# A two-part transformer layer on one core: another order of the same tasks, with the last token blocks loaded by SyncE

## The chip, the cores and the metric

The kernel runs on one core of a Trainium2 chip. A core has a matrix engine (TensorE, PE in the profile; its weight loads are shown apart as PEld), VectorE (DVE), ScalarE (ACT), GpSimd (POOL) and SyncE (SP), which only issues DMAs here. ACT issues some DMAs too. Each engine runs its own instructions strictly in their order; semaphores hold an instruction back until what it needs is there, and everything behind it on that engine waits too. Matmuls write to PSUM, which this kernel uses as eight banks of 128 x 512 f32. The metric is the device time of one execution in microseconds (us), lower is better.

## The reference

One sequence of 2048 tokens, width 640, all bf16. Part A is attention with a memory: layer norm, then q, k, v for 32 heads of 20; the tokens are cut into four segments of 512, and within a segment attention is causal.

```python
for s in range(N):                       # N = 4 segments of L = 512
    logits = einsum('bhqd,bhkd->bhqk', qs, ks) * scale + mask
    a_dot = einsum('bhqk,bhkd->bhqd', softmax(logits), vs)
    a_mem = einsum('bhld,bhde->bhle', phi(qs), M) / (einsum('bhld,bhd->bhl', phi(qs), z) + 1e-6)
    outs.append(g * a_mem + (1 - g) * a_dot)
    M = M + einsum('bhld,bhle->bhde', phi(ks), vs)
    z = z + einsum('bhld->bhd', phi(ks))
h = x + concat(outs) @ wo
out = h + silu(layernorm(h) @ w1) @ w2   # part B, 640 -> 1728 -> 640
```

Here phi(t) is t + 1 for positive t and exp(t) otherwise, and g is the sigmoid of one number for each head.

## The kernel before

The kernel declares 1,455 tasks (a group of matmuls, one copy, one DMA), each with what it reads and writes. Nothing is scheduled at run time. A long string, `ORDER`, lists the names of all tasks; `schedule` takes them one by one, and each is added to the end of the program of its engine. So the order of the list is, engine by engine, the order of the instructions. What the tasks of different engines owe each other (data and reused buffers) is turned into semaphore waits afterwards. A row of the list reads `name/engine:slots`: the letter after the stroke chooses the engine where there is a choice (A ACT, D DVE, G POOL, S SP), and the numbers choose the buffer, such as the PSUM bank. Two rules of the code matter:

```python
if name.startswith("fill"):
    ...
    t.name, t.eng, t.emit = "fill", PE, self.filler(a, int(name[4:]))
    order.append(t)
    continue
```

`fill30` puts thirty matmuls of 256 columns of zeros (L619) into PE's queue at that place. They read the zeros that `zpad` (L596, DVE) has written, and so wait for it, and nothing reads what they compute. They are no part of the declared tasks.

The segments are worked one after the other with overlap: while the scores of one segment are computed, the projections of the next and the second part of the one before run in between. Names carry the segment and the group or the block of 128 tokens. The ones that matter here:

- `x0`, `x1`, `x2`, `x4`, `x8`, `x12` (L579): loads of token blocks; `x12` loads the last four, into the buffers of blocks 0 to 3, when their outputs `out0` to `out3` (L1260) have been read out of them. `w_...` (L582): loads of weights.
- `iota` (L631, POOL) and `sel` (L633, DVE): the identity matrix, which the transposes on PE use.
- `n1_st`, `n1_r`, `n1_ap` (L747 and L750, L762 to L768, L774): statistics, inverse deviation and application of the first layer norm for a block. `n1_tp` (L783, PE) and `n1_te` (L792) transpose the first four blocks through PSUM; later blocks are transposed by DMA (`n1_tr`, L798). `n2_...`: the same for the second layer norm.
- `re_wq`, `re_wk` (L697 on ACT, L699 on DVE): one of five pieces of the query and key weights is put in the order of the heads.
- `pr` (L861, PE), `qe` (L869 on ACT, L870 on DVE): projections of queries and keys and their copies out of PSUM. `pr041x` is segment 0, piece 4, keys (1), first half (x). `ex` (L876), `pha` (L883) and `phb` (L889) make phi of them.
- `vt` (L901): twelve SBUF-to-SBUF DMAs for each segment, which gather the heads of groups 5 to 7; the scores of these groups need all twelve.
- `v` (L826) and `ve` (L836 on ACT, L837 on DVE): values.
- `qk` (L938, PE): scores of a group of four heads, `e` (L950, ACT): their exponential (four heads in one instruction in segment 0, two elsewhere), `mk` (L961, POOL): the causal mask.
- `av` (L982, PE), `oe` (L995 on ACT, L997 on DVE), `tn` (L1011, L1015), `nm` (L1028 to L1030 in segment 0, L1042 to L1048 later), `ad` (L1056): values times weights, copy, transposition back with the part from memory, division, and sum.
- `kt` (L1096), `mz` (L1104), `ma` (L1129 to L1133), `mb` (L1140): the update of the memory; `kt` is a transposing DMA issued by SP, into one of two buffers.
- `ot` (L1157), `wo` (L1165), `rs` (L1173): output projection and residual. `h1` (L1200, tail L1194), `th` (L1209), `s` (L1215), `h2` (L1242), `o` (L1255), `out` (L1260): the second part and the store.

Of the kernel before, what the change touches and what calls it, by code (L numbers as in the profile page):

```python
# [371 lines left out]
n1_st7:4 n1_st8:6 n1_r8/G n1_r7/D lsc2 lsc3 pr000y:4 qe000y/A qk3x0:0 e3x0:3 mk3x_0 vt02/A mk2x_256 vt05/S vt07/A
pr021y:7 qe021y/D pha031:1 epsg1 vt010/S vt011/S mk3x_256 pr020y:5 pr011y:6 qe011y/A vt04/S pr010y:4 qe010y/D qe020y/A
qk4x0:0 e4x0:5 mk4x_0 mk4x_256 phb031 n1_st11:2 vt06/A vt08/S vt09/S v00:6 ve00/A:0 qk0yb0:2 e0yb0:4 n1_st9:1
n1_st10:0 vt00/A vt03/S mk0yb_0 n1_tr5:0 kt00:1 n1_r11/D ex021:0 mk0yb_256 ex011:2 v01:0 qk1yb0:2 e1yb0:6 mk1yb_0
n1_r10/G ve01/D pha021:0 phb021 kt02:0 mk1yb_256 v03:6 ve03/D n1_ap11:2 n1_ap7:3 n1_tr7 n1_ap6:0 av4x:0 av0x:1
# [15 lines left out]
e8a0:6 av6y:4 pha111:1 e8a2 mk8a_0 oe6y/D:0 ex140:0 phb140 th0_8_0:0 qk8e0:0 e8e2:1 av4y:6 oe4y/D:1 mz03:7 e8e0
ma03/D:4 mk8e_0 mb03:0 mk8e_256 tn4y:6 nm4y:3 kt12:0 ex141:1 av7y:4 oe7y/D:1 tn6y:7 nm6y:0 qk8b0:0 e8b2:4 tn7y:4
nm7y:3 ot3 ot2 s0_8_0 pr130:6 qe130/D:0 e8b0 mk8b_0 mk8b_384 vt19/S pha130:0 qk9a0:2 e9a2:5 pr131:7 qe131/D vt12/S
vt11/S mz04:0 vt18/S n1_tr10:0 kt10:1 ma04/D:1 e9a0 mb04:0 mk9a_0 n1_tr8 vt110/S n1_tr11 h1_0_2_0:1 th0_2_0:1 vt15/S
qk9b0:4 e9b0:0 s0_2_0 pha131:0 h1_0_11_0:2 th0_11_0:0 s0_11_0 h1_0_0_0:0 th0_0_0:1 s0_0_0 e9b2 mk9b_0 h1_0_9_0:3
# [5 lines left out]
n2_st2:7 n2_r2/G qk12b0:1 e12b2:2 pr220:0 e12b0 qk13a0:3 qe220/D:0 mz13:7 ma13 n2_ap2:2 n2_tr2 e13a2:3 e13a0 mk13a_0
mk12b_0 mk12b_384 kt11:0 av11:2 tn9:0 v20:6 oe11/A:0 qk12e0:2 nm9:1,0 ve20/A:0 e12e0:0 mz10:0 kt14:1 e12e2 ma10
mk12e_0 ad9 n2_ap3:0 n2_tr3 v21:6 ve21/D qk13b0:0 e13b0:1 pr211:4 e13b2 mk13b_0 mk13b_384 pr210:5 qe211/D:0 ex211:2
mk12e_256 tn11:6 nm11:3,1 ad11 qe210/A qk14a0:1 e14a2:4 e14a0 mk14a_0 pr231:0 pha211:2 qe231/D:0 ex210:0 pr200:5
ex231:1 qk14b0:0 e14b2:6 e14b0 mk14b_0 mk14b_384 qe200/D:0 phb211 av13:4 oe13/D:0 ex200:2 v23:6 ve23/D h1_0_8_1:5
th0_8_1:1 qk14e0:0 e14e2:1 s0_8_1 mz11:4 ma11 e14e0 mk14e_0 mk14e_256 tn13:6 pr201:5 qe201/A tn10:2 pha200:0
h1_0_7_1:1 th0_7_1:0 nm13:3,1 ad13 mb10:0 qk15a0:4 e15a2:3 e15a0 mk15a_0 phb200 s0_7_1 pr221:0 qe221/A av14:1 av12:6
nm10:0,0 ad10 qk15b0:2 e15b2:4 vt20/S:0 vt26/S e15b0 mk15b_0 mk15b_384 vt29/S oe14/D:0 vt23/S tn14:0 oe12/D:1 nm14:3,0
pr241:7 qe241/D:0 pha201:1 mb11:0 ad14 ex201:2 h1_0_12_1:6 th0_12_1:1 qk16b0:0 e16b0:2 s0_12_1 tn12:4 nm12:0,1  # L410
h1_0_4_1:7 th0_4_1:0 s0_4_1 phb201 e16b2 mk16b_0 mk16b_384 h1_0_10_1:6 h1_0_0_1:0 av15:1 th0_0_1:1 s0_0_1 pha221:0
th0_10_1:0 s0_10_1 pha210:0 qk16a0:2 h1_0_6_1:7 oe15/A:0 tn15:0 mb13:0 ex221:2 phb221 kt22:0 e16a2:6 e16a0 ad12
nm15:0,0 ad15 ot6:0 ot7 ot4 pr240:6 h1_0_5_1:4 th0_6_1:0 qk16e0:0 mb12:0 qe240/D th0_5_1:1 s0_6_1 e16e0:5 s0_5_1 e16e2
mk16e_0 phb210 ex240:2 pha220:0 pha231:0 phb231 pr230:5 qe230/D vt25/S vt28/S ot5 vt27/S vt22/S pha240:0 vt210/S
vt211/S mk16a_0 vt21/S vt24/S mk16e_256 ex220:0 v22:6 ve22/D qk17b0:0 e17b2:3 phb240 h1_0_13_1:4 th0_13_1:1
h1_0_11_1:5 s0_13_1 th0_11_1:0 s0_11_1 phb220 e17b0 mk17b_0 mk17b_384 pha230:0 wo6:6 rs6 qk18b0:2 av16:0 oe16/D:1
# [901 lines left out]
```

## Time and profile before

| | us |
|---|---|
| median of 3 runs (lowest to highest) | 302.56 (302.05 to 302.67) |
| the profiled execution, own time | 303.2 |
| its span | 301.4 |
| ACT busy | 222.4 |
| POOL busy | 141.8 |

The span runs from the first to the last instruction of the profiled execution; 1.8 us of its time lie around it. A row of the timeline reads: start, length, engine and line, operation, tile written and tile read, shape, count, and in brackets how long the engine had been idle and what ended that. A row of waits reads: engine, tile and line, what released it, us in total, times, longest. ACTq and SPq are the queues in which those engines issue DMAs. `PT` is the tile of the exponentials, `stt` that of the statistics, `sT` that of the second part's activations (and, at first, of the raw weights); `w_sb` stands for several tiles of one shape in memory, the queries and keys of segment 0 among them.

### The profile page before, as it was taken

The numbers are of one execution on the slowest core, as the hardware profiler recorded it, in microseconds if no ns is written. First come the engines' busy times: TensorE is split into PE (matmuls) and PEld (weight loads), VectorE is DVE, ScalarE is ACT, GpSimd is POOL, SyncE is SP. The second block draws the span as 40 slices with busy tenths as digits, with TensorE's granted clock in tenths as the row PEclk, the third lists the DMA queues.
The fourth block names the chain that finished last, engine by engine and source line by source line (L and its number), as shares of the span: only waits on it lengthen the run. The fifth ranks groups of instructions, "written<-read, shape, count | busy, mean of one in ns | idle before, by whom it ended". The sixth has DMA issues, their size and how long they took to land.

```text
span 301.4 us, 7468 instructions
## 1 busy us (share of the span) xinstructions
PE 289.2 (96%) x2991; PEld 172.0 (57%) x3014; DVE 217.9 (72%) x510; ACT 222.4 (74%) x298; POOL 141.8 (47%) x272
## 2 busy tenths in 40 slices
...
GB/s 258 362 361 121 106 63 127 107 8 171 97 84 69 73 10 18 43 93 61 74 125 36 79 29 2 39 79 62 65 67 25 0 44 45 105 50 24 0 28 61
DMA packets 49250, 24.66 MB, mean 82 GB/s; under 512 B 39168, under 2 KB 47616, under 8 KB 49216
## 3 DMA queue, kind: packets, MB, share of 16 engines
...
## 4 chain that ended last, share of the span: by engine, by line
PE 75%; ACT 11%; DVE 5%; DMA 4%; issue 2%; SPq 1%; POOL 1%; ACTq 0%
PE ps_all L1242 21%; PE ps_all L1200 14%; PE ps_all L861 9%; ACT PT L950 8%; PE ps_all L1165 7%; PE ps_all L938 7%; PE ps_all L982 6%; PE ps_all L826 6%; DMA x_tok<-in_A_x_dram 3%; DVE stt L747 2%; PE ps_all L1011 2%; PE ps_all L1015 2%; SPq L901 1%; PE ps_all L1104 1%; DMA w_sb<-w_sb 1%
## 5 line engine op out<-in xcount | busy, mean ns | idle before, releaser
L950 ACT ACTIVATE PT<-ps_all 128x1024 bf16<-128x1024 f32 (+2 forms) x144 | 155.3, 1124 | 16.8 <-PE ps_all L938 15.7
L961 POOL TENSOR_SCALAR_AFFINE_SELECT PT<-PT 128x512 bf16<-128x512 bf16 x128 | 81.9, 645 | 70.5 <-ACT PT L950 67.6
L1242 PE MATMUL ps_all<-w_sb,sT 128*128 128x320 bf16 (+2 forms) x462 | 64.6, 295 | 0.0
L1200 PE MATMUL ps_all<-hT,w_sb 128*128 128x512 bf16 (+1 forms) x315 | 60.2, 335 | 1.0 <-issue 0.7
L1209 ACT ACTIVATE th<-ps_all 128x512 f32<-128x512 f32 (+2 forms) x70 | 33.6, 508 | 35.6 <-PE ps_all L1194 16.8
L1242 PEld LDWEIGHTS ps_all<-w_sb,sT 128*128 128x128 bf16 x462 | 43.1, 98 | 19.1 <-issue 3.0
L1215 DVE SCALAR_TENSOR_TENSOR sT<-th,ps_all 128x512 bf16<-128x512 f32 (+2 forms) x70 | 37.9, 561 | 18.5 <-ACT th L1209 17.8
L1200 PEld LDWEIGHTS ps_all<-hT,w_sb 128*128 128x128 bf16 x325 | 30.2, 98 | 25.3 <-issue 1.7
L1255 DVE SCALAR_TENSOR_TENSOR x_tok<-ps_all,x_tok 128x640 bf16<-128x640 f32 (+3 forms) x18 | 13.4, 749 | 23.1 <-PE ps_all L1242 23.0
L747 DVE BATCH_NORM_STATS2 stt<-x_tok 128x6 f32<-128x320 bf16 x64 | 27.9, 477 | 2.7 <-DMA x_tok<-in_A_x_dram 2.4
L1165 PE MATMUL ps_all<-wo_sb,oT 128*128 128x320 bf16 x160 | 24.1, 299 | 0.1
L982 PE MATMUL ps_all<-PT,Vx 128*32 128x256 bf16 (+3 forms) x576 | 23.5, 287 | 0.6 <-POOL PT L961 0.5
L1056 POOL TENSOR_TENSOR otok<-on 128x320 bf16<-128x320 bf16 x24 | 19.0, 792 | 5.9 <-DVE on L1048 5.8
L768 POOL TENSOR_TENSOR rst<-rst,eps_c 128x1 f32<-128x1 f32 x32 | 18.6, 583 | 5.6 <-DVE rst L762 3.8
L870 DVE CAST QK<-ps_all 128x512 bf16<-128x512 f32 x23 | 15.8, 686 | 6.9 <-PE ps_all L861 6.7
L1048 DVE TENSOR_TENSOR on<-ps_all,rd 128x640 bf16<-128x640 f32 x24 | 19.8, 825 | 0.8
L765 POOL TENSOR_TENSOR rst<-mvt,eps_c 128x1 f32<-128x1 f32 x23 | 4.9, 212 | 30.5 <-DVE mvt L750 28.1
L1165 PEld LDWEIGHTS ps_all<-wo_sb,oT 128*128 128x128 bf16 x160 | 14.9, 98 | 7.2 <-issue 1.9
L982 PEld LDWEIGHTS ps_all<-PT,Vx 128*32 128x32 bf16 x576 | 12.3, 96 | 10.9 <-issue 5.0
L826 PE MATMUL ps_all<-wv_sb,xT 128*128 128x320 bf16 x120 | 18.3, 299 | 0.1
L861 PE MATMUL ps_all<-xT,wqr 128*128 128x512 bf16 x71 | 17.7, 380 | 0.3 <-issue 0.2
L997 DVE TENSOR_SCALAR oTs<-ps_all,lsc 128x512 bf16<-128x512 f32 (+1 forms) x25 | 15.8, 640 | 2.9 <-PE ps_all L982 2.7
...
## 6 DMA issues: line engine op xcount, KB each, us to landing
...
out_dram<-x_tok SPq DMA_DIRECT2D x9, 160.0 KB, 1.8
...
out_dram<-x_tok ACTq DMA_DIRECT2D x6, 160.0 KB, 2.0
...
```

The source lines that it names most:

```text
L747: T.add(DV, lambda e, hh=hh: e.bn_stats(out=stt[:, s, 6 * hh:6 * hh + 6], in_=xb[:, 320 * hh:320 * hh + 320]), reads=R((xa, xsub)), writes ...
L826: fns.append(lambda e, c=c, hh=hh: e.matmul(bank(ps, hh)[:, 0:320], lhsT=xT_[:, c, 128 * i:128 * i + 128], rhs=wv_sb[:, c, 320 * hh:320 * ...
L861: fns = [lambda e, kc=kc: e.matmul(bank(ps)[:, lo:hi], lhsT=wt[:, kc, c, :], rhs=xT_[:, kc, lo:hi], start=(kc == 0), stop=(kc == NC - 1)) ...
L938: fns.append(lambda e, j=j, o=o, r=r, q0=q0, q1=q1, qa=qa, ka=ka: e.matmul(ps_all[:, o:o + q1 - q0], lhsT=ka[32 * r:32 * r + DH, 128 * j:1 ...
L950: T.add(AC, lambda e: e.activation(out=pt[:, pta.slot, q0:q0 + nq, 0:width], in_=sc3[:, b0:b0 + nq, 0:width], func=ACT.Exp, scale=SCALE), ...
L961: T.add(PO, lambda e: e.affine_select(out=v, in_=v, pattern=[[0, 4], [1, 128]], compare_op=ALU.is_ge, fill=0.0, base=0, channel_multiplier ...
L982: fns.append(lambda e, j=j, r=r, h=h, pa=pa, pt=pt, co=co, q0=q0, ji=ji: e.matmul(bank(po)[32 * r:32 * r + 32, q0:hi], lhsT=Vx[:, vx.slot, ...
L1165: fns.append(lambda e, c=c, hh=hh: e.matmul(bank(ps, hh)[:, 0:320], lhsT=oT[:, c, 128 * i:128 * i + 128], rhs=wo_sb[:, c, 320 * hh:320 * h ...
L1200: fns = [lambda e, c=c: e.matmul(bank(ps)[:, lo:hi], lhsT=w1_sb[:, c, 128 * f:128 * f + 128], rhs=hT[:, c, lo:hi], start=(c == 0), stop=(c ...
L1209: T.add(AC, lambda e: e.activation(out=th[:, tha.slot, lo:hi], in_=bank(ps)[:, lo:hi], func=ACT.Tanh, scale=0.5), reads=R((ps, [0])), writ ...
L1215: T.add(DV, lambda e: e.scalar_tensor_tensor(out=sT[:, f, lo:hi], in0=th[:, tha.slot, lo:hi], scalar=1.0, in1=bank(ps)[:, lo:hi], op0=ALU. ...
L1242: fns.append(lambda e, f=f, t0=t0, fr=fr, hh=hh, n=n: e.matmul(bank(pa, hh)[:, 0:n], lhsT=sT[:, f, t0:t0 + 128], rhs=w2_sb[:, fr, c0 + 320 ...
```

## The change

Only `ORDER` is replaced. Both lists hold the same 1,455 declared tasks, and both compute the exponential of segment 0 four heads at a time. What differs:

- the order, mostly by exchanges of near neighbours; on PE the largest moves are among the last blocks of the second part (`h2_9` to `h2_14`, and the `h1_3` tasks);
- the zero matmuls: 32, 15 and 4 instead of 30, 7 and 4; the second group stands ahead of `pr020x` instead of behind it;
- on DVE `sel` stands ahead of `zpad`; on POOL `mt2 halfc mt0 mta2 mtb2 mm10` stand ahead of `iota`, where `mt2 vpad1 mt1 vpad0 mt0` stood;
- the engine of 46 tasks: 15 go from ACT to DVE (`re_wk1`, `qe031x`, `qe000y`, `oe4x`, `oe0x`, `oe2x`, `ma00`, `qe210`, `qe301`, `qe341`, `qe340`, `ve31`, `oe25`, `oe26`, `oe30`), 12 from DVE to ACT (`re_wq3`, `qe030x`, `qe040y`, `qe031y`, `qe021y`, `ma02`, `qe241`, `oe18`, `ve30`, `qe300`, `qe331`, `oe27`), 9 between DVE and POOL (all `n1_r` or `n2_r`), and ten DMAs change their queue: `w_w2_0`, `w_w2_2`, `vt111`, `out0`, `out1`, `out2`, `x12`, `out11` from ACT to SP, `out5`, `out13` from SP to ACT.

Of the two lists, the rows at the start, those that the text speaks of, and the last two:

```diff
-zpad:0 x0:7 mt2 vpad1 mt1 vpad0 mt0 iota epsg0 mt3 halfc sel x1:3 mta3 epsc w_q:0 x2:5,0 w_k1 mta0 mtb0 w_k0 mtb3 mm2
-w_wv0:0 x4:1,2,4,6 w_wv1 warm n1_st0/D:1,0 n1_r0/G n1_st1/D:6 n1_r1/D n1_ap0:0 mm9 n1_ap1:1 n1_st2/D:2 n1_r2/G mta1
-mm8 re_wq2/D:0 n1_st3/D:0 n1_r3/G w2z/G:0 w_wo:0 beta w_w2_4 mm11 x8/S:8,9,10,11 mta2 mtb1 mtb2 mm5 mm3 re_wq0/D mm4
-mm10 w_w1_2:0 n1_ap2:3 mm6 mm1 re_wk0/D:0 w_w1_1 n1_ap3:2 re_wq4/D mm7 re_wq3/D re_wk3/D re_wk2/D fill30:0 n1_st5:3
-n1_r5/G mm0 n1_tp0:6 re_wk4/D n1_st4:7 n1_r4/G w_w1_0 w_w2_5 w_w1_3 n1_te0/A:0 n1_ap5:0 n1_tp1:4 n1_te1/A pr020x:2
-re_wq1/A fill7:1 pr010x:0 qe020x/A:0 re_wk1/A qe010x/A:0 w_w1_4 pr000x:4 qe000x/A:0 n1_tp2:5 n1_te2/A pr001x:7
-qe001x/A n1_tp3:2 n1_te3/A pr011x:1 qe011x/A qk0x0:4 e0x0:0 mk0x_0 pr040x:0 pr001y:2 qe001y/A pr030x:3 qe040x/A:0
...
-phb001 n1_st6:5 pr031y:3 pr041y:2 qe041y/A pr030y:0 qe030y/A qe031y/D ex031:0 pr041x:6 qe041x/D vt01/S:0 n1_r6/D
...
-oe4x/A:1 qk7x0:2 av2x:6 n1_tr4 tn4x:7 n1_r9/D oe0x/A:0 e7x0:5 n1_tr6 oe2x/A:1 nm4x:0 pha011:2 mk7x_0 mk7x_256 v02:0
...
-av1x:0 fill4:6 tn0x:7 av7x:6 oe7x/A:0 oe1x/D:1 tn1x:0 nm2x:1 qk0ya0:2 av5x:1 nm0x:0 nm1x:3 oe5x/D:1 av3x:7 tn7x:6
-nm7x:2 oe3x/D:0 av6x:1 tn5x:6 nm5x:3 mz00:0 tn3x:7 e0ya0:5 oe6x/A:1 qk1ya0:2 nm3x:1 tn6x:6 nm6x:0 ma00/A:0 mb00:0
-phb041 n1_ap8:0 ot1:0 v10:0 mz02:7 ot0 kt01:1 e1ya0:0 qk2ya0:2 ve10/A av0y:6 oe0y/D:1 ma02/D:3 n1_ap9:3 mb02:0 kt03:0
-e2ya0:2 v12:0 ve12/D qk2yb0:2 wo1:6 e2yb0:1 mk2yb_0 qk3ya0:0 e3ya0:3 w_w2_0/A av1y:4 oe1y/A:0 rs1 mk2yb_256 n2_st1:5
...
-s0_3_0 th0_10_0:0 s0_10_0 h1_0_1_0:4 qk7yb0:0 mk6yb_256 pr140:5 qe140/D e7yb0:2 w_w2_2/A w_w2_3/S th0_1_0:1 s0_1_0
...
-mk9b_384 vt17/S mz12:1 ma12 vt111/A h1_0_13_0:2 th0_13_0:0 th0_9_0:1 s0_9_0 qk10a0:4 e10a0:3 s0_13_0 n1_tr9 e10a2
...
-mk11b_0 mk11b_384 phb111 h2_1_2 h2_1_3 o1 qk12a0:0 av10:4 wo2:5 out0/A e12a0:5 oe10/D:1 e12a2 ad8:0 mk12a_0 out1/A rs2
...
-mk19b_0 n2_tr4 mk19b_384 mk18a_0 h2_2_1 h2_2_2 h2_2_3 o2 h2_3_0:0 tn17:2 nm17:3,1 n2_tr5 ad17:0 qk19a0:4 out2/A
...
-tn18:0 nm18:2,0 ad18 mz14:7 ma14 mb14:0 kt23:1 h1_1_10_0:6 tn16:4 oe19/A:0 th1_10_0:0 x12/A s1_10_0:0 nm16:2,1
...
-out15_1/A h2_12_2 h2_12_3 o12 out12/S h2_14_3 o14 out14/S h2_15_0_0:2 h2_15_1_0 h2_13_0:0 h2_13_1 h2_13_2 h2_13_3 o13
-out13/S h2_15_2_0 h2_15_3_0 o15_0 out15_0/S h2_15_0_2:3 h2_15_1_2 h2_15_2_2 h2_15_3_2 o15_2 out15_2/S
+x1:3 x0:7 mt2:0 halfc mt0 mta2 mtb2 w_q:0 mm10 iota mt1 mta0 mtb0 mm2 mm4 x2:5,0 w_k1 w_k0 w_wv1:0 sel zpad warm vpad0
+epsc n1_st0/D:1,0 n1_r0/G n1_st1/D:6 n1_r1/D mm6 n1_ap0:0 n1_ap1:1 epsg0 n1_st2/D:2 n1_r2/G re_wq2/D:0 mt3 mta3
+n1_st3/D:0 n1_r3/G w2z/G:0 mtb3 mm8 mm11 w_wv0 x4:1,2,4,6 mta1 w_wo:0 beta w_w2_4 x8/S:8,9,10,11 w_w1_2:0 mm0 mtb1 mm5
+n1_ap2:3 re_wq0/D mm3 re_wk0/D:0 mm9 w_w1_1 mm1 vpad1 n1_ap3:2 w_w1_4 w_w2_5 re_wk1/D re_wq4/D re_wk2/D re_wk3/D
+re_wk4/D n1_st4:7 n1_r4/G n1_st7:4 n1_r7/G n1_st6:5 n1_r6/G mm7 n1_st5:3 n1_r5/G w_w1_0 fill32:0 n1_tp0:2 n1_te0/A:0
+n1_tp1:0 n1_te1/A fill15:4 re_wq1/A w_w1_3 pr020x:0 re_wq3/A pr010x:6 qe020x/A:0 n1_tp2:2 qe010x/A:0 n1_ap4:1 n1_te2/A
+pr000x:5 qe000x/A:0 pr001x:1 qe001x/A n1_tp3:6 pr011x:4 qk0x0:0 n1_ap7:3 n1_ap6:0 n1_te3/A qe011x/A pr040x:5 e0x0:0
+mk0x_0 mk0x_256 qe040x/A:0 pr001y:6 pr030x:7 qe001y/A qk1x0:0 e1x0:1 zf0 zf1 mzc9 mzc8 mzc0 mzc11 mzc1 mzc5 mzc3 mzc6
+mzc2 pr021x:4 qe021x/A pr031x:5 lsc0 mzc4 lsc1 pr040y:6 qe040y/A mk1x_0 qk2x0:0 qe030x/A:0 qe031x/D e2x0:2 mk2x_0
+mk1x_256 mk2x_256 pr030y:4 pr031y:6 qe031y/A pr041y:7 mzc7 pr041x:0 qe030y/A qe041y/A qe041x/D pha031:1 ex001:1
+pha001:2 vt011/S:0 ex031:0 n1_ap5:2 phb031 pr000y:1 qe000y/D qk3x0:2 e3x0:3 vt02/A mk3x_0 mzc10 epsg1 n1_st8:6 vt08/S
...
+n1_tr6 qk1yb0:2 e1yb0:6 ex021:0 kt00:1 ve03/D n1_r8/D mk1yb_0 mk1yb_256 n1_tr4 av0x:1 av4x:0 oe4x/D:1 tn4x:6 av2x:7
+oe0x/D:0 qk7x0:2 e7x0:5 mk7x_0 nm4x:0 phb021 kt02:0 mk7x_256 n1_ap9:2 oe2x/D:1 n1_tr7 v02:0 qk5x0:2 e5x0:0 mk5x_0
+mk5x_256 ve02/D v11:6 tn2x:0 qk6x0:1 e6x0:2 mk6x_0 pha011:2 mk6x_256 n1_ap11:0 phb011 ve11/D:1 av1x:5 oe1x/D:1 fill4:6
+nm2x:1 tn0x:6 av7x:7 tn1x:5 nm0x:0 qk0ya0:0 nm1x:3 mz00:4 oe7x/A:0 pha041:0 kt01:1 ma00/D:0 mb00:0 av5x:6 av3x:7
+tn7x:5 oe5x/D:1 tn5x:4 av6x:6 e0ya0:5 oe3x/D:0 tn3x:7 nm7x:2 oe6x/A:1 qk1ya0:0 nm5x:3 nm3x:1 tn6x:6 nm6x:0 ot1:0 v10:4
...
+e2yb0:1 wo1:6 w_w2_0/S mk2yb_0 mk2yb_256 qk3ya0:0 e3ya0:3 ve12/D av1y:4 oe1y/A:0 rs1 n2_st1:5 n2_r1/G tn0y:7 nm0y:1
...
+qk7yb0:0 w_w2_2/S w_w2_3/S pr140:6 s0_3_0 e7yb0:2 mk7yb_0 mk7yb_256 pha110:0 h1_0_6_0:4 th0_1_0:1 th0_6_0:0 qe140/D
...
+pha130:0 e8b0 mk8b_0 mk8b_384 qk9a0:2 e9a2:5 pr131:6 qe131/D vt14/S n1_tr10:0 vt18/S vt111/S vt11/S n1_tr11 n1_tr9
...
+h2_1_0:6 e10e0 ex110:0 kt13:0 o0 out0/S mk10e_0 phb110 qk11a0:0 e11a0:6 e11a2 mk11a_0 mk10e_256 wo3:4 ex111:2 rs3
...
+av10:4 oe10/D:1 pha111:2 n2_ap3:0 out1/S n2_tr3 wo2:6 e12a0 mk12a_0 rs2 phb111 qk12b0:2 e12b2:2 pr220:0 qe220/D:0
...
+e18a0:4 e18a2 mk18a_0 n2_ap5:3 n2_tr5 h2_2_1 h2_2_2 qk19b0:0 e19b2:3 e19b0 mk19b_0 h2_2_3 o2 out2/S h2_3_0:4 mk19b_384
+ad17:0 qk19a0:0 e19a2:2 e19a0 mk19a_0 h2_3_1 h2_3_2 h2_3_3 av18:7 oe18/A:0 qk20b0:0 o3 out3/S e20b0:5 e20b2 mz14:6
+ma14 mb14:0 mk20b_0 mk20b_384 kt23:1 tn18:4 av19:7 oe19/A:0 x12/S h1_1_10_0:6 th1_10_0:0 nm18:2,0 s1_10_0:0 pha241:0
...
+out13/A h2_14_0:6 h2_14_1 h2_14_2 h2_14_3 o14 out14/S h2_15_0_2:5 h2_15_1_2 h2_15_3_1 o15_1 out15_1/A h2_15_2_2
+h2_15_3_2 o15_2 out15_2/S
```

More of the change, by code (lines that the diff above doesn't have):

```diff
@@ L372 @@
[L372 to L376, printed above, removed]
@@ L392 @@
[L392 to L396, printed above, removed]
@@ L402 @@
[L402 to L416, printed above, removed]
@@ L422 @@
-e19a2:2 e19a0 mk19a_0 h2_3_1 h2_3_2 h2_3_3 o3 out3/S av18:7 qk20b0:3 e20b2:5 av19:2 e20b0 mk20b_0 mk20b_384 oe18/D:0
-tn18:0 nm18:2,0 ad18 mz14:7 ma14 mb14:0 kt23:1 h1_1_10_0:6 tn16:4 oe19/A:0 th1_10_0:0 x12/A s1_10_0:0 nm16:2,1
-qk21b0:0 e21b0:6 pha241:0 e21b2 ad16 mk21b_0 h1_1_4_0:7 h1_1_7_0:6 th1_4_0:0 s1_4_0 th1_7_0:1 s1_7_0 phb241 n1_st12:0
-n1_r12/G n1_st13:3 n1_r13/G qk20a0:2 e20a2:0 e20a0 mk20a_0 h1_1_12_0:1 th1_12_0:0 h1_1_1_0:0 th1_1_0:1 s1_1_0 qk20e0:4
-h1_1_5_0:3 e20e2:4 e20e0 mk20e_0 mk21b_384 mk20e_256 n1_ap12:1 n1_tr12:0 s1_12_0 th1_5_0:1 h1_1_11_0:2 th1_11_0:0
@@ new lines @@
+mk1x_256 mk2x_256 pr030y:4 pr031y:6 qe031y/A pr041y:7 mzc7 pr041x:0 qe030y/A qe041y/A qe041x/D pha031:1 ex001:1
+pha001:2 vt011/S:0 ex031:0 n1_ap5:2 phb031 pr000y:1 qe000y/D qk3x0:2 e3x0:3 vt02/A mk3x_0 mzc10 epsg1 n1_st8:6 vt08/S
+lsc2 vt04/S vt05/S phb001 lsc3 mk3x_256 pr020y:6 pr021y:7 qe021y/A qe020y/A pha021:0 pr011y:0 qe011y/A qk4x0:2 e4x0:5
+mk4x_0 pr010y:1 qe010y/D vt07/A mk4x_256 n1_st11:2 n1_st10:0 vt01/S vt00/A v00:6 n1_st9:1 ve00/A:0 qk0yb0:2 vt010/S
+e0yb0:4 vt09/S mk0yb_0 vt06/A n1_r11/G ex041:1 mk0yb_256 ex011:2 vt03/S v01:0 ve01/D n1_r9/D n1_tr5:0 n1_r10/D v03:6
```

124 lines of the change are left out of this document (72 added, 52 removed).

## The prediction

> **What bounds the kernel now.** I read the page's totals first, then the busy time by stretches, then who TensorE (PE) waited for in three stretches, and last the timeline of the first 20 us and of the places where PE waits.
>
> ```profile
> span 301.4 us, 7468 instructions
> PE 289.2 (96%) x2991; PEld 172.0 (57%) x3014; DVE 217.9 (72%) x510; ACT 222.4 (74%) x298; POOL 141.8 (47%) x272
> ...
> 13.00:42.00 29.00, 26.95 (x353) 17.41 (x351) 26.18 (x85) 27.69 (x40) 22.06 (x54) 1.00 0.70 184
> 42.00:82.00 40.00, 38.14 (x458) 21.94 (x460) 29.93 (x79) 38.30 (x46) 17.24 (x28) 1.00 0.45 102
> 82.00:150.00 68.00, 67.14 (x752) 39.77 (x759) 54.17 (x120) 61.23 (x84) 38.96 (x63) 1.00 0.36 59
> 150.00:170.00 20.00, 18.83 (x166) 8.80 (x170) 17.04 (x39) 17.34 (x24) 10.83 (x20) 1.00 0.30 71
> 170.00:302.00 132.00, 127.76 (x1204) 76.00 (x1206) 81.70 (x157) 71.40 (x95) 43.24 (x71) 1.00 0.21 44
> ```
>
> The rows by stretch give length, then busy time of PE, PEld, DVE, ACT, POOL. PE is the bound nearly everywhere: 96% of the span, and the same matmuls stand in both lists, the zero matmuls of the fills apart. So a new order can win only what PE now spends waiting, and can lose without limit. From 13 to 42 ACT (27.69 of 29.00) and DVE (26.18) run almost without a break beside PE; from 42 to 82 ACT does (38.30 of 40.00). The waits of PE, in the order 13 to 42 (two rows), 42 to 82 (one), 82 to the end (three):
>
> ```profile
> PE ps_all L938 <- DMA w_sb<-w_sb: 0.7, 1, 0.7
> PE ps_all L982 <- POOL PT L961: 0.5, 1, 0.5
> ...
> PE ps_all L938 <- ACT PT L950: 1.0, 4, 0.4
> ...
> PE ps_all L1104 <- DVE sT L1215: 0.9, 1, 0.9
> PE ps_all L1200 <- issue: 0.7, 4, 0.2
> PE ps_all L861 <- issue: 0.5, 3, 0.2
> ```
>
> What can be won after the head is thus about 0.7 + 0.5 + 1.0 + 0.9 = 3.1 us; the "issue" rows have no releaser and stay.
>
> **The head (0 to 20 us): a loss.** The new list puts `sel` (L633) ahead of `zpad` (L596) on DVE. `sel` waits for POOL's `iota`; the fills (L619) read `zpad`. Today's rows:
>
> ```profile
> 0.88 0.17 DVE L596 MEMSET zpad<- 128x128 uint32 x1 [0.88 <-PEq L1303]
> 1.11 5.66 PE L619 MATMUL ps_all<-zpad 128*128 128x256 bf16 x30 [1.11 <-DVE zpad L596]
> 2.44 0.23 POOL L631 IOTA iot<- 128x128 int32 x1
> 2.71 0.23 DVE L633 TENSOR_SCALAR ident<-iot 128x128 bf16<-128x128 int32 x1 [1.66 <-POOL iot L631]
> ...
> 1.10:5.34 4.24, 4.23 (x20) 3.00 (x21) 1.00 0.83 271
> ...
> 6.61 0.44 PE L783 MATMUL ps_all<-ident,xn_rot 128*128 128x128 bf16 x5
> 7.09 0.70 ACT L792 ACTIVATE hT<-ps_all 128x640 bf16<-128x640 f32 x1 [2.73 <-PE ps_all L783]
> 8.55 0.82 ACT L697 ACTIVATE wqr<-sT 128x400 bf16<-128x400 bf16 x2
> 8.87 0.71 PE L861 MATMUL ps_all<-hT,wqr 128*128 128x256 bf16 x5 [0.95 <-DVE wqr L699]
> 9.41 0.93 PE L619 MATMUL ps_all<-zpad 128*128 128x256 bf16 x7
> 10.18 1.25 PE L861 MATMUL ps_all<-hT,wqr 128*128 128x256 bf16 x10
> 11.12 0.73 ACT L869 ACTIVATE w_sb<-ps_all 128x256 bf16<-128x256 f32 x2
> 13.37 0.34 PE L938 MATMUL ps_all<-w_sb 20*128 20x256 bf16 x8
> 13.79 1.46 ACT L950 ACTIVATE PT<-ps_all 128x1536 bf16<-128x1536 f32 x1
> 18.08 1.45 ACT L950 ACTIVATE PT<-ps_all 128x1536 bf16<-128x1536 f32 x1
> 20.03 0.75 DVE L870 CAST w_sb<-ps_all 128x256 bf16<-128x256 f32 x2
> ```
>
> A fill costs 4.24 / 20 = 0.212 us until about 5.6 us, and later (9.41 to 10.18 for seven) 0.110 us: TensorE's clock is at half speed for its first 4.5 us of work, 1.11 to about 5.6. (The granted clock in that row, third from its end, reads 1.00 all the same; the spacing decides.) Ahead of `iota` POOL has seven operations today and six of like size in the new list, so `sel` stays near 2.5 to 2.7, `zpad` ends near 2.8, and the 32 fills start at 2.8 instead of 1.11. They stand ahead of the first transpose n1_tp0 (L783, now at 6.61) in PE's queue. Lower bound: the clock rises at the same instant as now, 5.6: 13 slow fills (2.8) and 19 fast (2.1) end at 7.7. Upper: all 32 are slow, 2.8 + 6.8 = 9.6. I take the middle by the nearest row, a slow stretch of the same 4.5 us: 21 slow (4.5), 11 fast (1.2), so n1_tp0 at 8.5, which is 1.9 us late.
>
> Behind it ACT copies both transposes (0.70 each), rearranges wqr (0.82, and re_wq3, of three pieces where today's has two, some 0.9 more), and copies four projections and a transpose (0.35 a projection from 0.73 for two): qk0x0, the first scores (L938), follows n1_tp0 by about 5.3 us, at 13.8 instead of 13.37. The second fill (15 instead of 7, 1.65 us) moves ahead of pr020x; it ends near 10.4, only 0.2 behind the second copy, and so costs next to nothing more. The third exponential, e2x0 (now 18.08 to 19.53), follows qk0x0 by three exponentials, a transpose copy, six projection copies and two small constants, some 7.0 us: it ends near 20.8, 1.3 us late. pr041x takes a bank from it, DVE's qe041x (the second cast of the 20.03 row, over at 20.78) ends near 22.0, and the SBUF copies `vt` (L901), which need it, start about 1 us late.
>
> From there to 42 us DVE is the tight engine. It was idle 29.00 - 26.18 = 2.8 us; the list gives it oe4x, oe0x, oe2x, ma00, re_wk1, qe031x and qe000y from ACT and takes re_wq3, qe030x, qe040y, qe031y and qe021y from it: net two more of about 0.4 to 0.5 us, 1 us, beside the 0.9 that it waits for qe041x. What is late next is v10, for whose PSUM banks PE needs DVE's nm5x:
>
> ```profile
> 39.39 1.52 PE L826 MATMUL ps_all<-wv_sb,xT 128*128 128x320 bf16 x10
> ```
>
> I put it at 40.4: **+1.0 us at 40 us**, bounds +0.2 (fills end at 7.7) and +2.1 (at 9.6). In this the repairs of this stretch are contained: av2x and tn4x go ahead of qk7x0 (which has the 0.7 of DMA wait), mz00 and tn5x ahead of av6x (the 0.5 for POOL); both only pass on a wait that grows. [...]
>
> **42 to 82 us: a gain.** ACT sets the pace here. The chain that ended last holds two pieces on it that are no arithmetic: the issue of w_w2_2 and that of vt111.
>
> ```profile
> 66.69 0.91 issue
> ...
> 79.15 0.40 ACTq L901
> ```
>
> Both go to SP (w_w2_0 and vt111 too; SP has room, its next work there is the `vt` copies of segment 1, some us later). That frees 0.91 + 0.40 = 1.3 us of ACT, but PE waits only 1.0 us for ACT's exponentials in the whole stretch, and two of the four waits lie ahead of 66 us. **-0.5 us**, bounds -1.0 and 0.
>
> **150 to 170 us, the last token blocks (x12): a gain.**
>
> ```profile
> 150.86 0.37 SPq L1260 DMA_DIRECT2D out_dram<-x_tok  x1
> 152.50 1.21 SPq L1096 DMA_TRANSPOSE phiKt<-phiK  x1
> ...
> 150.89 0.73 PE L982 MATMUL ps_all<-PT,Vx 128*32 128x512 bf16 x16
> 151.87 0.61 PE L1104 MATMUL ps_all<-Vx,phiKt 128*128 128x84 bf16 x8
> ...
> 153.60 0.40 ACTq L579 DMA_DIRECT2D x_tok<-in_A_x_dram  x1
> ...
> 159.79 0.89 DVE L747 BATCH_NORM_STATS2 stt<-x_tok 128x6 f32<-128x320 bf16 x2 [1.47 <-DMA x_tok<-in_A_x_dram]
> ...
> out_dram<-x_tok SPq DMA_DIRECT2D x9, 160.0 KB, 1.8
> ```
>
> On ACT x12 stands behind two exponentials and oe19 and is issued at 153.60. It may not go before out3, which reads the same buffers, has landed: 150.86 + 1.8 = 152.7. On SP it stands behind the transposing DMA kt23, which waits for mz14; mz14 (L1104) goes ahead of av19 (L982) and tn18 in PE's queue, by 151.87 - 150.89 = 1.0 us, so kt23 runs from about 151.5 to 152.7. Then x12 is issued at 152.8, 0.8 us earlier; DVE's wait of 1.47 shrinks to 0.7, and the 0.9 us that PE waits for DVE's sT behind it (mz23) nearly goes. **-0.8 us**, bounds -0.9 and 0 (kt23 not earlier: 152.50 + 1.21 = 153.71, as late as now). Behind x12 on SP stands n1_tr12, which needs x12 anyway.
>
> **The rest.** out0, out1 and out2 leave ACT, where PE hardly waits for it (82 to 150: PE 67.14 of 68.00 busy): nothing; without that cover 0.4 us each. The two lists end on the same last piece of block 15, its output on SP: nothing. In 82 to 302 a few hundred neighbours are exchanged; the waits they can open are not in the trace. From both sides: nothing, or as much as today's list shows between 13 and 42, 1.2 us and more; the row nearest is that this list, of the same kind, has 1.2 us of short gaps beside mz23 there. I take **+0.5**, with -0.3 to +1.3.
>
> Sum: +1.0 - 0.5 - 0.8 + 0.5 = +0.2 us. On the profiled execution, 303.2 us (span 301.4 and 1.8 around it), that is 303.4; it lies 0.6 above the median of the three runs shown, so against that median I forecast 302.56 + 0.2 = **302.8 us**: no change that can be told (0.2%, 0.6 us, is about what a measurement of this kernel can tell).
>
> **The rivals.** *The late clock loses more, and the list gives nothing back* (slower). Place: PE's queue at n1_tp0; the fills run slow to the end, +2.1 at 40 us; ACT's relief comes to nothing as DVE stays late (0), x12 gives -0.5: +1.6, and 304.2 us. It decides from a first transpose at about 9 us on. For it: nothing but `zpad` starts the fills, DVE has no room until 42 us. Against it: the slow stretch of 4.5 us. *The head costs almost nothing* (faster): clock up at 5.6, +0.2, ACT -1.0, x12 -0.9, the rest 0: -1.7, and 300.9 us. For it: PE waited 0.95 us for wqr at 8.87 and spent 0.77 on seven fills behind it, cover for a late start. Against it: PE would have to be left with almost no wait. *The x12 move does nothing*, since kt23 stays in front of it on SP: the forecast without -0.8, 303.6 us. For it the 1.21 us of kt23; against it mz14's earlier place.
>
> **Chances.** Forecast 0.42 (its own range 302.0 to 303.8: no change 0.24, slower 0.12, faster 0.06); first rival 0.25, all slower; second 0.23 (faster 0.22, no change 0.01); third 0.10 (slower 0.06, no change 0.04). Together faster 0.28, within 0.2% 0.29, slower 0.43. The range takes in both sides, 300.9 to 304.6.
>
> **What would show it.** The first fill at 2.8, n1_tp0 at 7.7 to 9.6 and the first scores at 13.4 to 15; v10 near 40.4. In 42 to 82 a smaller wait of PE for ACT's PT; x12 issued by SP at 152.8 plus the shift of that place, and the wait of L1104 for sT under 0.2. I am wrong if the fills start at 1.1, if PE's place at 40 us is unchanged though the fills are late, or if new waits of over 1.3 us stand after 82.

## The result, and the profile after

| | median, us (lowest to highest) | beside the kernel before, same chips | ratio, 95% |
|---|---|---|---|
| before | 302.23 (301.80 to 303.51), 7 runs | | |
| changed | 304.45 (303.52 to 305.21), 7 runs | +2.22 us | 1.0071 [1.0048, 1.0094] |

The changed kernel is slower, by 0.7%. 304.45 us lies in the predicted range, 300.9 to 304.6, which takes in the rivals too, but only 0.15 us from its end, and the prediction does not work that end out. It lies outside the 302.0 to 303.8 that the prediction gives its own forecast: 302.8 us and no change was wrong. The first rival's 304.2 us is nearer, partly by luck: of its reasons, fills that run slow to the end and 0.5 us won by x12 did not come.

The page's totals, then the busy time by stretches (length, then PE, PEld, DVE, ACT, POOL, granted clock, DMA share, GB/s) of the changed kernel:

```profile
span 302.7 us, 7496 instructions
PE 289.4 (96%) x3002; PEld 172.6 (57%) x3024; DVE 220.4 (73%) x509; ACT 220.9 (73%) x296; POOL 142.5 (47%) x275
```

```profile
42.00:82.00 40.00, 37.84 (x474) 21.78 (x477) 30.83 (x79) 38.41 (x47) 15.68 (x27) 1.00 0.49 94
82.00:150.00 68.00, 66.56 (x747) 39.19 (x749) 54.32 (x119) 62.03 (x85) 38.34 (x64) 1.00 0.31 59
```

PE is busy 37.84 of the 40 us and 66.56 of the 68, against 38.14 and 67.14 before: both stretches, the one where ACT was relieved too, have more gaps than they had.

The waits of PE, from 13.3 to 42 us (two rows), 42 to 82 (one) and 82 to the end (one):

```profile
PE ps_all L619 <- DVE Vx L837: 1.1, 1, 1.1
PE ps_all L1015 <- DVE oTs L997: 1.0, 2, 0.8
...
PE ps_all L938 <- ACT PT L950: 0.4, 1, 0.4
...
PE ps_all L1165 <- DVE Vx L837: 0.7, 1, 0.7
```

Before 42 us PE now waits for DVE, 1.1 us for a copy of values (L837) and 1.0 us for two copies of attention results (oTs, L997), where it waited for a DMA and for POOL before. The wait for ACT's exponentials from 42 to 82 is down from 1.0 to 0.4 us as foreseen, but that gained nothing there. Behind 82 us there is one new wait of over 0.3 us, for DVE's copy of values (L837), ahead of L1165. The wait of L1104 for sT is gone. The head, in the timeline:

```profile
2.06 0.23 POOL L631 IOTA iot<- 128x128 int32 x1
2.33 0.23 DVE L633 TENSOR_SCALAR ident<-iot 128x128 bf16<-128x128 int32 x1 [2.33 <-POOL iot L631]
2.53 0.17 DVE L596 MEMSET zpad<- 128x128 uint32 x1
2.75 5.83 PE L619 MATMUL ps_all<-zpad 128*128 128x256 bf16 x32 [2.75 <-DVE zpad L596]
8.42 0.72 PE L783 MATMUL ps_all<-ident,xn_rot 128*128 128x128 bf16 x10
14.00 0.34 PE L938 MATMUL ps_all<-w_sb 20*128 20x256 bf16 x8
...
21.07 0.42 DVE L870 CAST w_sb<-ps_all 128x256 bf16<-128x256 f32 x1 [0.92 <-PE ps_all L861]
...
41.00 1.52 PE L826 MATMUL ps_all<-wv_sb,xT 128*128 128x320 bf16 x10
```

The fills start at 2.75, the transposes at 8.4, the first scores at 14.0, qe041x ends at 21.5 and v10 (the last row) starts at 41.0. Two profiled executions cannot be set against each other as they are, though: that of before (303.2 us) lies 1 us above its kernel's median, and experiments 4 and 5 show what was in it.

### The profile page after: what moved, and what is told of

Same layout as the page of the kernel before. It is cut to its first block, busy times and chain, and to the rows that moved or that the text cites. A ratio compares the mean times of both kernels' runs of the same rounds, so it can differ in the third digit from the quotient of the medians.

```text
span 302.7 us, 7496 instructions
## 1 busy us (share of the span) xinstructions
PE 289.4 (96%) x3002; PEld 172.6 (57%) x3024; DVE 220.4 (73%) x509; ACT 220.9 (73%) x296; POOL 142.5 (47%) x275
## 4 chain that ended last, share of the span: by engine, by line
PE 80%; ACT 9%; DVE 7%; issue 2%; POOL 1%; POOLq 0%; ACTq 0%
PE ps_all L1242 20%; PE ps_all L1200 15%; PE ps_all L861 11%; PE ps_all L938 7%; PE ps_all L1165 7%; ACT PT L950 7%; PE ps_all L982 6%; PE ps_all L826 5%; PE ps_all L619 3%; PE ps_all L1011 2%; PE ps_all L1015 1%; PE ps_all L1104 1%; DVE Vx L837 1%; ACT th L1209 1%; DVE stt L747 1%
## 5 line engine op out<-in xcount | busy, mean ns | idle before, releaser
L1200 PE MATMUL ps_all<-hT,w_sb 128*128 128x512 bf16 (+1 forms) x315 | 61.0, 336 | 1.1 <-issue 0.7
L1215 DVE SCALAR_TENSOR_TENSOR sT<-th,ps_all 128x512 bf16<-128x512 f32 (+2 forms) x70 | 37.8, 559 | 17.2 <-ACT th L1209 16.5
L747 DVE BATCH_NORM_STATS2 stt<-x_tok 128x6 f32<-128x320 bf16 x64 | 27.8, 476 | 1.5 <-DMA x_tok<-in_A_x_dram 1.2
L1165 PE MATMUL ps_all<-wo_sb,oT 128*128 128x320 bf16 x160 | 24.1, 299 | 1.0 <-DVE Vx L837 0.7
L870 DVE CAST QK<-ps_all 128x512 bf16<-128x512 f32 x24 | 16.5, 688 | 6.3 <-PE ps_all L861 6.2
L997 DVE TENSOR_SCALAR oTs<-ps_all,lsc 128x512 bf16<-128x512 f32 (+1 forms) x29 | 17.7, 623 | 3.7 <-PE ps_all L982 3.5
L1165 PEld LDWEIGHTS ps_all<-wo_sb,oT 128*128 128x128 bf16 x160 | 14.8, 98 | 8.6 <-issue 3.2
L774 DVE TENSOR_SCALAR xn_rot<-x_tok,mvt,rst 128x640 bf16<-128x640 bf16 x32 | 15.3, 487 | 5.6 <-POOL rst L768 5.3
L861 PE MATMUL ps_all<-xT,wkr 128*128 128x512 bf16 x68 | 17.2, 380 | 1.0 <-issue 0.5
```

Of the source, the lines that this page charges most:

```text
L747: T.add(DV, lambda e, hh=hh: e.bn_stats(out=stt[:, s, 6 * hh:6 * hh + 6], in_=xb[:, 320 * hh:320 * hh + 320]), reads=R((xa, xsub)), writes ...
L861: fns = [lambda e, kc=kc: e.matmul(bank(ps)[:, lo:hi], lhsT=wt[:, kc, c, :], rhs=xT_[:, kc, lo:hi], start=(kc == 0), stop=(kc == NC - 1)) ...
L1165: fns.append(lambda e, c=c, hh=hh: e.matmul(bank(ps, hh)[:, 0:320], lhsT=oT[:, c, 128 * i:128 * i + 128], rhs=wo_sb[:, c, 320 * hh:320 * h ...
L1200: fns = [lambda e, c=c: e.matmul(bank(ps)[:, lo:hi], lhsT=w1_sb[:, c, 128 * f:128 * f + 128], rhs=hT[:, c, lo:hi], start=(c == 0), stop=(c ...
L1215: T.add(DV, lambda e: e.scalar_tensor_tensor(out=sT[:, f, lo:hi], in0=th[:, tha.slot, lo:hi], scalar=1.0, in1=bank(ps)[:, lo:hi], op0=ALU. ...
```

## The experiments

Differences in time are taken against runs of the kernel before on the same chip: 301.94 us (median of 11) beside the first four, 302.14 beside the others (15, then 23 runs). Two theories stood at first: H, the late fills make the loss of the first 40 us; D, DVE's own list between 20 and 42 us makes it.

**1. `zpad` to the front of the changed list.**

```diff
-x1:3 x0:7 mt2:0 ... sel zpad warm
+zpad:0 x1:3 x0:7 mt2 ... sel warm
```

> The changed list with zpad alone moved back to the front of DVE's program, so that the fills start near 1.1 us and not 2.75. Theory H (the late fills make the loss of the first 40 us): the first transpose near 6.8 instead of 8.31, DVE's wait of 0.9 us for pr041x goes, v10 starts near 40.0 instead of 40.97, and the time falls by about 0.9 us, to 303.5. Theory D (DVE's own load between 20 and 42 us makes it): the head is earlier, but v10 stays within 0.2 of 40.97 and the time within 0.3 of 304.45.

304.01 us, +2.07 (1.0062 [1.0050, 1.0075]). The time lies between the two bands. The first scores are 0.59 us earlier than in the changed kernel, v10 only 0.15. In this list, then, something behind the head binds as well.

**2. Three statistics and two applications of the first norm, some 4 us of DVE's list, behind nm6x (40 us).** Their transposes are issued only after 80 us.

```diff
-n1_st11 n1_st10 ... n1_st9 ... n1_r11/G ... n1_r9/D ... n1_r10/D ... n1_ap9 ... n1_ap11
 ... nm6x:0
+n1_st11 n1_st10 n1_st9 n1_r11/G n1_r10/D n1_r9/D n1_ap9 n1_ap11
```

> The changed list with the layer norm statistics of blocks 9, 10 and 11 (n1_st, n1_r) and the applications n1_ap9 and n1_ap11, not needed before 70 us, moved from behind qe010y to behind nm6x: about 3 x 1.05 + 2 x 0.4 = 4 us less for DVE ahead of nm5x; the head stays late. Theory D: DVE no longer binds, v10 falls to where PE's own path puts it, 0.5 to 0.8 us behind the kernel before, near 40.0, and the time falls by about 0.9 us. Theory H: v10 and the time stay within 0.3.

307.15 us, +5.21 (1.0168 [1.0153, 1.0184]). Both expectations missed the time; the trace says why. v10 starts at 39.66, 1.3 us earlier than in the changed kernel, as D would have it. But now DVE's timeline reads:

```profile
40.40 0.88 DVE L747 BATCH_NORM_STATS2 stt<-x_tok 128x6 f32<-128x320 bf16 x2
...
44.71 1.01 DVE L774 TENSOR_SCALAR xn_rot<-x_tok,mvt,rst 128x640 bf16<-128x640 bf16 x2 [1.01 <-POOL rst L768]
45.64 0.41 DVE L889 TENSOR_TENSOR phiK<-phiK,ex 128x512 bf16<-128x512 bf16 x1
45.98 0.47 DVE L997 TENSOR_SCALAR oTs<-ps_all,lsc 128x256 bf16<-128x256 f32 x1
```

and PE's waits from 42 to 50 us:

```profile
PE ps_all L1165 <- DVE oTs L997: 2.6, 1, 2.6
```

The block stands ahead of oe0y (L997), with a wait for POOL of 1.01 us in it; oe0y starts at 45.98 instead of 43.69, and wo1 waits for it. The work went out of one tight place into the next one. That explains half of the loss against the changed kernel: wo1 starts 1.3 us later than there. The other half arises inside wo1 and just behind it. Its row in PE's timeline, and the granted clock of the whole profile in 40 slices (the seventh runs from 45.8 to 53.4 us):

```profile
46.71 2.82 PE L1165 MATMUL ps_all<-wo_sb,oT 128*128 128x320 bf16 x10 [2.55 <-DVE oTs L997]
```

```profile
PEclk9999997999999999999999999999999999999999
```

These ten matmuls take 2.82 us where the same ten of other pieces take 1.52; the granted clock reads 7 tenths in the seventh slice and 9 (90% or more) in all others, 0.994 on the mean of the execution, and from 50 us on everything is 2.6 us later than in the changed kernel. In the profile of the next run PE waits 2.55 us at the same place and the mean clock is 1.000. Of the executions of run 2, three have a mean clock of 0.994 and one of 1.000, the fastest (306.56 us). So the same wait stands beside a lower clock in one profile and beside the full one in the other; what brought the clock down stays open.

**3. Both, and ve22 moved forward** (pha230, pha231 and phb231 behind ve22 on DVE): the edits of 1, 2 and 7 together.

> The changed list with three repairs: zpad first, the statistics later, and pha230, pha231, phb231 moved behind ve22 on DVE (the wait of PE for ve22 at wo6, 0.7 us). If the losses are separate and additive: v10 near 39.2, wo6 no longer 0.9 us late, and 304.45 - 0.9 - 0.9 - 0.8 = about 301.9. If the last two bind one after the other on the same work, only about 1 us comes back: 303.3.

306.89 us, +4.95 (1.0153 [1.0137, 1.0170]): both expected times and v10 (40.36) missed. The same block at 40 us holds wo1 back by the same 2.6 us, and behind wo6 a new wait of 1.2 us appears, of which run 7 shows the cause.

**4. The kernel before with `zpad` behind `sel`**, the head of the change alone.

```diff
-zpad:0 ... mt2 ... sel
+... mt2:0 ... sel zpad
```

> The kernel before with one thing of the change: zpad behind sel on DVE. The fills start near 3.0. Theory H: the first transpose falls from 6.57 to about 8.3, the third exponential is about 1 us late, v10 0.6 to 1.0 us late, the time 0.6 to 1.0 us up. Theory D: DVE of this list has the room (it waits 0.6 us between 13 and 42), v10 at most 0.3 us late and the time within 0.3.

303.28 us, +1.34 (1.0036 [1.0023, 1.0049]), above even H's band: for the list of before, the late fills alone cost over 1 us. Its timeline of PE:

```profile
3.14 5.96 PE L619 MATMUL ps_all<-zpad 128*128 128x256 bf16 x30 [3.14 <-DVE zpad L596]
...
10.77 0.72 PE L861 MATMUL ps_all<-hT,wqr 128*128 128x256 bf16 x5 [1.11 <-ACT hT L792]
...
40.99 1.52 PE L826 MATMUL ps_all<-wv_sb,xT 128*128 128x320 bf16 x10
```

Against the first profile of before v10 is 1.6 us late (H had 0.6 to 1.0), and so is every later piece up to 161 us; then, at mz23, 1.2 us of it vanish, with x12 where it was. That spoke against the term for x12. Theory X: x12 lands late because it is issued late. Theory L: it landed late in that one profiled execution of before.

**5. The kernel before, unchanged, profiled a second time.**

> The kernel before, unchanged, profiled a second time. Theory X (as predicted): its wait of 0.9 us ahead of mz23 comes from the late issue of x12 and returns in every execution: x12 lands about 6.2 us after its issue, n1_st12 starts at 159.8, mz23 at 162.5, span 301.4. Theory L (a slow landing in that one execution): x12 lands 4.4 to 4.7 us after its issue as in the other profiles, mz23 starts 1.2 us earlier at 161.3, span 300.1 to 300.3, and the profiled execution takes about 302.0.

301.83 us, span 300.1: L. The load of x12 in the view of the transfers (size, us from issue to landing), in the first profile and in the second:

```profile
x_tok<-in_A_x_dram ACTq DMA_DIRECT2D x1, 640.0 KB, 6.2
```

```profile
x_tok<-in_A_x_dram ACTq DMA_DIRECT2D x1, 640.0 KB, 4.3
```

In the second profile's timeline, its issue on ACT's queue, DVE's n1_st12 (the L747 row), and PE's mz23:

```profile
153.55 0.40 ACTq L579 DMA_DIRECT2D x_tok<-in_A_x_dram  x1
...
157.86 0.42 DVE L889 TENSOR_TENSOR phiK<-phiK,ex 128x512 bf16<-128x512 bf16 x1
158.20 0.88 DVE L747 BATCH_NORM_STATS2 stt<-x_tok 128x6 f32<-128x320 bf16 x2
...
161.43 0.59 PE L1104 MATMUL ps_all<-Vx,phiKt 128*128 128x252 bf16 x4
```

The issue is at the same place (153.55 against 153.60), the transfer lands after 4.3 us instead of 6.2, n1_st12 follows its neighbour without a wait, and the span is 1.3 us shorter. In twelve of the thirteen profiles of this study x12 lands after 4.3 to 4.7 us, from ACT or SP; 6.2 us stands in the first profile of before alone.

**6. The changed kernel with x12 on ACT.**

```diff
-oe19/A:0 x12/S
+oe19/A:0 x12/A
```

> The changed kernel with x12 issued by ACT again, as before the change. Theory X: the issue comes 1 us later, the wait ahead of mz23 is back, +0.9 to +1.25 us on the changed kernel's 304.45, so about 305.5. Theory L: the landing after 4.4 to 4.7 us leaves mz23 where it is, 304.2 to 304.8.

304.94 us, +2.80 (1.0105 [1.0074, 1.0136]), a little over L's band and below X's figure. The landing takes 4.4 us. Against the second profile of before this one is 2.06 us late at v10 and 3.12 at mz23, so 1.06 between; in the changed kernel these are 1.65, 2.68 and 1.03. Moving x12 to SP is thus worth 0.03 us in these two profiles. The issue did not come 1 us later, as expected: it stands at 155.57, which is the changed kernel's 155.15 and the 0.4 us by which this execution is late. So this run does not test a later issue; it shows that the queue makes no difference to it. What separates the two profiles arises at 23.0 us: one small operation of DVE (L653) takes 0.64 us instead of 0.20, and DVE, and from 27.4 us on PE, are 0.4 us late from there. Why it took longer stays open.

**7. The changed kernel with pha230, pha231, phb231 behind ve22**, for the new wait at wo6. DVE and PE in the changed kernel's timeline:

```profile
130.19 0.72 DVE L883 TENSOR_SCALAR phiK<-QK 128x512 bf16<-128x512 bf16 x1
130.94 0.80 DVE L889 TENSOR_TENSOR phiK<-phiK,ex 128x512 bf16<-128x512 bf16 x1
131.67 0.81 DVE L837 CAST Vx<-ps_all 128x640 bf16<-128x640 f32 x1
...
132.62 1.52 PE L1165 MATMUL ps_all<-wo_sb,oT 128*128 128x320 bf16 x10 [0.67 <-DVE Vx L837]
```

The list of before has the two phi operations ahead of qe230, so that ve22 (L837) runs earlier against its matmuls and wo6 does not wait.

```diff
-pha230:0 pha231:0 phb231 v22:6 ... ve22/D
+v22:6 ... ve22/D pha230:0 pha231:0 phb231
```

> The changed kernel with pha230, pha231 and phb231 behind ve22 on DVE. If ve22 waits behind these three and for nothing else, wo6 starts at 131.7 instead of 132.6 and the kernel takes 303.6 (-0.85). If ve22 waits for its own matmuls, or what follows takes the gain back, 304.2 to 304.7.

304.90 us, +2.76 (1.0092 [1.0078, 1.0106]), a little over the second band. wo6 no longer waits, but the wait moves on by one piece. PE's timeline:

```profile
132.63 1.52 PE L1165 MATMUL ps_all<-wo_sb,oT 128*128 128x320 bf16 x10
135.33 0.40 PE L938 MATMUL ps_all<-QK 20*128 20x384 bf16 x8 [1.18 <-DVE sT L1215]
```

qk18b0 takes its bank from s0_11_1 (L1215), which now stands behind the four phi operations.

**8. A repaired list**: `zpad` first, ve22 early as in 7, and the statistics in idle places of DVE.

```diff
+... phb041 n1_st11:2 n1_r11/G ... ve12/D n1_st10:0 n1_r10/D ... n2_ap1:3 n1_ap11:0
+... s0_4_0 n1_st9:1 n1_r9/D ... s0_6_0 n1_ap9:2
```

> The changed kernel with zpad first, ve22 early, and the three statistics n1_st11, n1_st10, n1_st9 and their two copies spread over idle places of DVE between 42 and 72 us instead of one block at 40 us. Theory D2 (fills and DVE's list bound the first 40 us one after the other; the earlier run with the statistics behind nm6x lost because they stood ahead of oe0y): v10 starts at 39.4 to 39.8, wo1 at 43.8 to 44.2, wo6 within 0.5 of the kernel before, the whole 302.0 to 302.6. If something else than these three makes the loss: above 303.3.

303.61 us, +1.47 (1.0055 [1.0034, 1.0076]): above 303.3, so by the expectation something else is in the loss, too. v10 is back to 40.07 and wo1 to 44.49, both 0.3 us behind their bands; behind them the wait of 1.2 us at qk18b0 is in it, as in 7, and that is made by the edit itself.

**9. The same with a better order around ve22**: pha231 and phb231 ahead of qe230, pha230 and phb220 behind s0_11_1.

```diff
-pr230:5 qe230/D ... ve22/D pha230:0 pha231:0 phb231 ... phb220 s0_13_1 s0_11_1
+pr230:5 pha231:0 phb231 qe230/D ... ve22/D ... s0_13_1 s0_11_1 pha230:0 phb220
```

> The repaired kernel of the run before, with a better order around ve22: pha231 and phb231, whose exponential has stood ready for 20 us, ahead of qe230; pha230 and phb220 behind s0_11_1. If s0_11_1 behind the four phi operations is what held qk18b0 and so gave the 1.2 us at wo7, wo6 and wo7 both start within 0.9 us of the second look at the kernel before (131.0 and 133.5 or earlier), and the kernel takes 302.2 to 302.6. If another wait takes its place: 303.2 or more.

302.83 us, +0.69 (1.0014 [1.0000, 1.0027]), a little over the expected band. wo6 starts at 130.60, wo7 at 133.52, within 0.9 us of the second profile of before. Of the 2.22 us, 1.5 are regained by moving DVE tasks in the list, `zpad` among them.

**10. The same as 9 with w_w2_0, w_w2_2 and vt111 on ACT again**, at their places in the new list.

```diff
-w_w2_0/S ... w_w2_2/S ... vt111/S
+w_w2_0/A ... w_w2_2/A ... vt111/A
```

> The same kernel as g1 with w_w2_0, w_w2_2 and vt111 issued by ACT again, as before the change. If taking these three from ACT was worth the 0.5 us of the prediction, +0.4 to +0.6 on g1, most of it by 65 us. If ACT is not what sets the pace of TensorE there, within 0.2 of g1.

304.18 us, +2.04 (1.0079 [1.0057, 1.0101]), 1.35 us slower than 9: more than either expected, and not by 65 us, where it stands 0.4 us ahead of 9, as at v10. The loss falls on two pieces. At 68.3 us the lead of 0.4 is gone: ACT issues w_w2_2 from 66.39 to 66.76, the next exponential starts at 66.82 although its scores are there, and PE waits 0.3 us for it. The larger piece follows in ACT's timeline:

```profile
77.43 0.73 ACTq L901 DMA_DIRECT2D QKV<-QK  x1
78.20 1.02 ACT L950 ACTIVATE PT<-ps_all 128x1024 bf16<-128x1024 f32 x1 [1.43 <-DVE Mz L1130]
```

and PE's waits from 76 to 131 us:

```profile
PE ps_all L1200 <- ACT PT L950: 1.3, 1, 1.3
```

vt111, a DMA issue on ACT, stands ahead of e9a0; it goes out right behind DVE's qe131, whose result it gathers, and e9a0 and with it h1_0_11_0 start late. At its place in this list vt111 cannot stay on ACT. Its issue costs 1.3 us, that of w_w2_2 some 0.35.

**11. The kernel before with the statistics spread as in 8.**

> The kernel before, with its own n1_st11, n1_st10, n1_st9 and the copies n1_ap11, n1_ap9 spread over the same idle places of DVE after 40 us. If the 20 to 42 us stretch of the kernel before is also held by DVE, v10 starts 0.3 to 0.5 us earlier than at 39.3 and the kernel takes 301.6 to 301.8. If it is held by TensorE's own work there, v10 stays within 0.1 us and the time within 0.3 of 302.1.

302.25 us, +0.11 (1.0013 [1.0001, 1.0026]), v10 at 39.29: within 0.03 us of before. In that list DVE has room for them between 20 and 42 us. No version beat the kernel before.

## Where the prediction held and where it failed, step by step

The table sets each term beside the shift of PE's pieces against the second profile of before (start of a piece's first weight load, us).

| piece | before, second profile | changed | shift | the stretch's term: measured, forecast |
|---|---|---|---|---|
| qk0x0 | 13.27 | 13.99 | +0.73 | |
| v10 | 39.32 | 40.97 | +1.65 | head to 40 us: +1.65, +1.0 |
| mz04 | 75.72 | 77.45 | +1.73 | 42 to 82: +0.1, -0.5 |
| wo6 | 130.07 | 132.59 | +2.52 | |
| mz23 | 161.22 | 163.90 | +2.68 | x12: 0.03 at most, -0.8 |
| end of span | 300.1 | 302.7 | +2.6 | the rest, from mz04 on: +0.9, +0.5 |

The sum was forecast at +0.2 and is +2.6 in these two profiles, +2.22 in the medians.

**150 to 170 us, the step that failed outright.** The prediction read the DVE wait of 1.47 us for x12 as a property of the list and priced an earlier issue at -0.8. The issue did come earlier against its surroundings, by 1.1 us (SP at 155.15, where this place is 2.7 us late), but the new order did that and not the queue (run 6). And the wait was a transfer that took 6.2 us instead of 4.3, in one execution (run 5), and the move is worth nothing: 0.03 us (run 6). The prediction noted that this execution lay 0.6 us above the median, then worked out a sum on it and carried the sum over: the term removed the very wait that set the execution above the median. Without it the same sum gives +1.0, and 303.6 us. The third rival had the x12 move at nothing and 303.6 us, but for another reason, kt23 ahead of it on SP.

**The head: right mechanism, too small.** `zpad` behind `sel`, fills from 2.75 (forecast 2.8), n1_tp0 at 8.31 (8.5), first scores at 13.99 (13.8): right. That n1_tp0 came so near is in part luck, since the slow stretch of the fills takes 4.5 us in this profile, but 5.9 and 2.6 in two others with the same head (last section). The first rival's fills, slow to the end, did not come. v10, forecast at 40.4 with an upper bound of 41.5, came at 40.97. Of the 0.6 us that the forecast lacks there, 0.2 lie ahead of the first scores; the mis-sized term is what follows, DVE's. From qk0x0 to v10 the kernels before (the first profile, the second, runs 4 and 11) take 25.99 to 26.06 us; with the new list (changed, runs 1, 6, 7) 26.98 to 27.42; with the statistics moved away (runs 2, 3, 8, 9, 10) 26.13 to 26.52. So the new list costs 0.9 to 1.4 us there whatever the head does; the forecast had 40.4 - 13.8 = 26.6, or +0.6. It set one more microsecond of DVE work and the wait for qe041x against 2.8 us of idle time, as if that idle time lay where it was needed. Busy time from 21 to 42 us in the second profile of before, the changed kernel and run 9:

```profile
21.00:42.00 21.00, 19.09 (x265) 11.75 (x262) 18.36 (x58) 19.67 (x25) 15.52 (x30) 1.00 0.55 115
```

```profile
21.00:42.00 21.00, 18.43 (x244) 11.21 (x242) 20.16 (x61) 17.98 (x21) 16.77 (x38) 1.00 0.52 114
```

```profile
21.00:42.00 21.00, 19.13 (x260) 11.55 (x256) 16.90 (x50) 18.46 (x21) 14.81 (x32) 1.00 0.52 112
```

The third column behind the length is DVE: 18.36, 20.16, 16.90. At 20.16 of 21 it is the bound, and PE's column, the first, falls. PE's wait at the third group of fills shows the same: 1.1 us for DVE's copy of values in the changed kernel and in runs 1, 6 and 7, and in run 9, as in before and in all runs with the statistics moved away:

```profile
PE ps_all L619 <- DVE Vx L837: 0.2, 1, 0.2
```

That also explains run 1: of a head 0.59 us earlier, 0.15 us arrive.

**42 to 82 us: the relief of ACT bought nothing on the whole.** The smaller wait for ACT came (0.4 us, against 1.0 in the first profile of before and 0.7 in the second), and PE's place did not move (+0.1, forecast -0.5). The step that failed is that a smaller wait for ACT is a gain for PE: in the changed kernel PE waits 0.5 us for DVE in this stretch, where both profiles of before show no wait for it; that these waits took up the gain is not tested. Run 10 splits the relief: w_w2_2 on SP is worth some 0.35 us in the repaired list, and vt111 in the new list's place 1.3 us, but that only undoes what the place would cost.

**The rest.** The forecast was +0.5, bounds -0.3 to +1.3; it is +0.9, of which 0.8 arise at wo6 and are explained by DVE's order there (runs 7 to 9). Where the other 0.1 goes stays open, and so does how the 0.69 us that run 9 still lacks could be regained. PE's wait for oTs ahead of 42 us stands in run 9 too (0.9 us); no run moves it.
